# A one-time ScalarE delay between the first store and the first refill of a four-slot streaming kernel

## The chip, the cores and the metric

The kernel runs on one core of a Trainium2 chip. The metric is the device time of one execution in microseconds; lower is better. Most executions of one kernel agree within 0.3%, and faster or slower needs 2%. No other core of the chip is used by the program.

## The reference, cut to what matters

The input `x` has 384 x 384 positions of 384 bf16 channels, 113.25 MB. A mean over all positions gives one value per channel; it is scaled by one weight and passed through a sigmoid, and every position is multiplied by the result.

```python
g = jnp.einsum("bhwc->bc", x) / (H * W)
s = g * w1d[0]              # k = 1, so no neighbours
s = _sigmoid(s)
return x * s[:, None, None, :]
```

Read literally, this needs `x` twice. The kernel reads it once: it takes the gate from the first 4 row groups (`s_early`), applies it at once, and sums everything on the side. At the end it compares the true bf16 gate with the early one; only if they differ does it do a second pass. They don't differ on this data. So 113.25 MB come in and 113.25 MB go out.

## The kernel before

A row group ("row" in the code) is 128 positions, one per partition of SBUF, the core's on-chip memory. A tile is 60 rows: 46,080 contiguous bytes on each of 128 partitions, 5.90 MB. There are 19 tiles and 4 slots for them in SBUF, plus 12 first rows kept apart. Loads are issued by SyncE (queue SPq), three half tiles at the start by ScalarE; all stores are issued by ScalarE (queue ACTq). TensorE sums each tile, then VectorE multiplies it in place, then it is stored, then its slot is loaded again. Each load or store is carried by 16 DMA engines in packets, for a full tile one packet per partition; it has landed when the last of the 16 engines has reported its part.

```python
    def put(place, n, r0, to=None):
        ...
        plan.op("vector", gate(to, place, n, s_early),
                reads=["s_early"] + rows(place, n), writes=rows(to, n))
        plan.final.append(
            plan.dma("scalar", dram(o_rows, r0, n), at(to, n), reads=rows(to, n))
        )
    ...
    for k in range(n_tiles):
        if k >= SLOTS:
            put(slot(k), TILE, row0(k - SLOTS))
            load(slot(k), TILE, row0(k))
        there = rows(slot(k), TILE)
        plan.relay(ready, "gpsimd", "tensor", there, there, ["acc1"])
    ...
    for k in range(n_tiles - SLOTS, last):
        put(slot(k), TILE, row0(k))
    put(slot(last), TILE, row0(last), slot(n_tiles))
    put(base, FIRST, 0)
```

`Planner` notes who writes and reads each row and adds the semaphore waits; each engine's stream keeps the order of the calls. I call the tiles 0 to 18, "store 3" the store of tile 3, "load 4" the load of tile 4, which is the first refill of a slot.

Of the kernel before, what the change touches and what calls it, by code (L numbers as in the profile page):

```python
# [3 lines left out]
P = 128  # L4
# [5 lines left out]
ACT_F = mybir.ActivationFunctionType  # L10
# [139 lines left out]
def split(n, most):  # L150
    k = -(-n // most)
    return [n // k + (i < n % k) for i in range(k)]
# [2 lines left out]
WIDE = 512  # L155


FIRST, EARLY, TILE, SLOTS, BOTH = 12, 4, 60, 4, 3


def bass_standalone__channel_attn_eca__vision_kernel(
# [5 lines left out]
    B, H, W, C = x.shape  # L167
    assert B == 1 and C == ROW and (B * H * W) % (4 * P) == 0
    n_rows = B * H * W // P
    x_rows, o_rows = x.flatten_outer_dims(), out.flatten_outer_dims()  # L170

    def dram(view, r0, n):
        return view[r0 * P : (r0 + n) * P, :].rearrange("(p t) c -> p (t c)", p=P)
# [5 lines left out]
    warm = nc.alloc_sbuf_tensor("warm", [P, 2], F32)  # L179
# [3 lines left out]
    n_arena = nc.sbuf_bytes_remaining // (2 * C)  # L183
# [7 lines left out]
    def at(r0, n):  # L191
        assert r0 + n <= n_arena
        return arena[:, r0 * C : (r0 + n) * C]

    def rows(r0, n):
        return [("sb", r) for r in range(r0, r0 + n)]

    def gate(to, place, n, s):
        s_b = s[:].unsqueeze(1).broadcast_to([P, n, C])
        v, to_v = (at(r, n).rearrange("p (t c) -> p t c", t=n) for r in (place, to))  # L200
        return lambda e: e.tensor_tensor(to_v, v, s_b, ALU.mult)  # L201

    n_tiles = (n_rows - FIRST) // TILE
    base = SLOTS * TILE
    assert (n_rows - FIRST) % TILE == 0 and base + FIRST < n_arena
    assert FIRST % 4 == EARLY % 4 == TILE % 4 == 0 and EARLY + 4 < FIRST
    last = n_tiles - 1
    ready = nc.alloc_semaphore("ready")
# [1 line left out]
    def slot(k):  # L210
        return k % SLOTS * TILE

    def row0(k):
        return FIRST + k * TILE
# [2 lines left out]
    s_true = at(base + FIRST, 1)  # L217
    plan = Planner(nc, "a", 70)

    def load(place, n, r0, queues=("sync",)):  # L220
        i = 0
        for queue, m in zip(queues, split(n, -(-n // len(queues)))):
            plan.dma(
                queue,
                at(place + i, m),
                dram(x_rows, r0, n)[:, i * C : (i + m) * C],
                writes=rows(place + i, m),
            )
            i += m
# [83 lines left out]
    def put(place, n, r0, to=None):  # L313
        to = place if to is None else to
        plan.op(
            "vector",
            gate(to, place, n, s_early),
            reads=["s_early"] + rows(place, n),
            writes=rows(to, n),
        )  # L320
        plan.final.append(
            plan.dma("scalar", dram(o_rows, r0, n), at(to, n), reads=rows(to, n))
        )

    def weight():

        plan.op(
            "scalar",
            lambda e: e.activation(warm[:, 1:2], warm[:, 0:1], ACT_F.Sigmoid),  # L329
            reads=["warm"],  # L330
            writes=["warm1"],
        )
        plan.op(
            "tensor",
            lambda e: e.matmul(  # L335
                w_all[:, 0:1], ones[0:1, :], w_one[0:1, 0:1], start=True, stop=True
            ),
            reads=["ones", "w_one"],
            writes=["w_all"],
        )  # L340
        for i, n in enumerate((EARLY, n_rows)):
            plan.op(
                "vector",
                lambda e, i=i, n=n: e.tensor_scalar_mul(  # L344
                    w_scaled[:, i : i + 1], w_all[:, 0:1], 1.0 / float(P * n)
                ),
                reads=["w_all"],
                writes=[f"w_scaled{i}"],
            )

    plan.op("gpsimd", lambda e: e.memset(warm[:, 0:1], 0.0), writes=["warm"])  # L351
    plan.op("vector", lambda e: e.memset(ones[:], 1.0), writes=["ones"])  # L352
    load(base, FIRST, 0)
    for k in range(BOTH):
        load(slot(k), TILE, row0(k), ("sync", "scalar"))
        if k == 0:
            plan.dma("scalar", w_one[0:1, 0:1], w1d.unsqueeze(0), writes=["w_one"])
    for k in range(BOTH, SLOTS):
        load(slot(k), TILE, row0(k))
    heads = {e: len(plan.streams[e]) for e in ("sync", "scalar")}  # L360
    weight()
    sum_first()
    add_banks(0, copy=True)
# [5 lines left out]
        reads=["total", "w_scaled0", "warm1"],  # L369
        writes=["s_early"],  # L370
# [3 lines left out]

    for k in range(n_tiles):
        if k >= SLOTS:
            put(slot(k), TILE, row0(k - SLOTS))
            load(slot(k), TILE, row0(k))
        there = rows(slot(k), TILE)
        plan.relay(ready, "gpsimd", "tensor", there, there, ["acc1"])  # L380
    plan.signals("tensor", rows(base, FIRST), ["acc1"])
    for k in range(n_tiles - SLOTS, last):
# [12 lines left out]
        reads=["total", "w_scaled1"],  # L395
        writes=["s_true"],
# [6 lines left out]
        reads=["s_true", "s_early"],  # L403
        writes=["total"],
# [4 lines left out]
        reads=["total"],  # L409
        writes=["wrong"],  # L410
# [4 lines left out]
        reads=["wrong"],  # L415
        writes=["redo"],
# [5 lines left out]
    half, r0 = base // 2, 0  # L422
    for k, n in enumerate(split(n_rows, half)):
        place = k % 2 * half
# [4 lines left out]
            reads=rows(place, n),  # L429
            writes=rows(place, n),  # L430
# [98 lines left out]
```

## Time and profile before

| | before |
|---|---|
| time, median of the first 3 runs | 529.54 us (529.05 to 530.78) |
| span of the profiled run | 527.2 us |
| PE busy, VectorE busy | 42%, 46% |
| DMA engines, share of 16 | 53.6% + 46.1% = 99.7% |
| bytes over the span | 226.52 MB, 430 GB/s |

From the page of the kernel before: the busy share of the 16 DMA engines in 40 slices (tenths), the rate in each slice, the two queues (q10 is ACTq, q1 is SPq: packets, MB, share of 16 engines' span), and the two large groups of DMA issues (last column: median us from issue to landing).

```profile
DMA  9999999999999999999999999999999999999997
GB/s 392 425 425 414 440 447 427 413 447 444 434 409 447 444 434 409 447 444 434 416 437 447 437 413 437 447 441 409 437 447 444 409 434 447 444 416 427 442 447 331
q10 hardware_dynamic: 3314, 122.10, 53.6%
q1 hardware_dynamic: 2880, 104.40, 46.1%
...
out_dram<-arena ACTq DMA_DIRECT2D x19, 5760.0 KB, 49.4
arena<-in_x_dram SPq DMA_DIRECT2D x16, 5760.0 KB, 35.6
```

The engines have work in every slice. The table by stage of the same kernel (start:end, length, then per engine busy us and count, granted clock, DMA share, GB/s) shows the long middle:

```profile
125.00:480.00 355.00, 149.17 (x585) 0.00 (x0) 158.17 (x14) 0.00 (x0) 0.00 (x0) 0.70 1.00 434
```

PE is busy for 149 of these 355 us and VectorE for 158; DMA has a share of 1.00. The trace also keeps a record of each DMA packet and of each DMA engine's part of a landing; I worked the following out of those packet records. A packet of 46,080 bytes takes 1.70 us, 27.07 B/ns, or 433 GB/s for 16 engines. At that pace all the bytes need 523 us. The Trainium skill ("DMA: Bandwidth & Descriptors", section "Where 436 GB/s comes from") gives 16 x 32 B x 850 MHz = 435.2 GB/s as the ceiling of the ports; the trace agrees, at 433.

The place that the change touches is 60 to 100 us. From the timeline of the kernel before (start, duration from the first to the last of a merged group, engine, operation):

```profile
61.72 31.48 ACTq L109 DMA_DIRECT2D out_dram<-arena  x3
...
75.00 24.42 SPq L109 DMA_DIRECT2D arena<-in_x_dram  x2
```

Store 0 lands at 74.98 us and load 4 is issued at 75.00. Store 1 was issued at 61.72 and is queued behind store 0.

### The profile page before, as it was taken

The numbers are of one execution on the slowest core, as the hardware profiler recorded it, in microseconds if no ns is written. First come the engines' busy times: TensorE is split into PE (matmuls) and PEld (weight loads), VectorE is DVE, ScalarE is ACT, GpSimd is POOL, SyncE is SP. The second block draws the span as 40 slices with busy tenths as digits, with TensorE's granted clock in tenths as the row PEclk, the third lists the DMA queues.
The fourth block names the chain that finished last, engine by engine and source line by source line (L and its number), as shares of the span: only waits on it lengthen the run. The fifth ranks groups of instructions, "written<-read, shape, count | busy, mean of one in ns | idle before, by whom it ended". The sixth has DMA issues, their size and how long they took to land. (4 is left out here: it accounts for less than half of the span.)

```text
span 527.2 us, 1066 instructions
## 1 busy us (share of the span) xinstructions
PE 220.1 (42%) x865; PEld 0.2 (0%) x2; DVE 240.1 (46%) x38; ACT 2.7 (1%) x4; POOL 0.3 (0%) x5
## 2 busy tenths in 40 slices
PE   0389471080807161625343343526261708080900
PEld 0000000000000000000000000000000000000000
DVE  0229958008090808171625353443536261708940
ACT  1000000000000000000000000000000000000000
POOL 0000000000000000000000000000000000000000
PEclk9999876586757676676869595858585858585865
DMA  9999999999999999999999999999999999999997
GB/s 392 425 425 414 440 447 427 413 447 444 434 409 447 444 434 409 447 444 434 416 437 447 437 413 437 447 441 409 437 447 444 409 434 447 444 416 427 442 447 331
DMA packets 6196, 226.52 MB, mean 430 GB/s; under 512 B 690, under 2 KB 690, under 8 KB 690
## 3 DMA queue, kind: packets, MB, share of 16 engines
q10 hardware_dynamic: 3314, 122.10, 53.6%
q1 hardware_dynamic: 2880, 104.40, 46.1%
q8 instruction: 1, 0.02, 0.0%
q14 instruction: 1, 0.01, 0.0%
HBM read 113.25 MB, written 113.25 MB: 430 GB/s over the span
## 5 line engine op out<-in xcount | busy, mean ns | idle before, releaser
L201 DVE TENSOR_TENSOR arena<-arena,s_early 128x23040 bf16<-128x23040 bf16 (+1 forms) x20 | 233.5, 11679 | 250.4 <-PE acc L237 247.0
L237 PE MATMUL acc<-arena,ones 128*128 128x512 bf16 x863 | 219.6, 421 | 265.5 <-PEq L276 265.5
L344 DVE TENSOR_SCALAR w_scaled<-w_all 128x1 f32<-128x1 f32 x2 | 0.2, 153 | 14.5 <-PE w_all L335 14.5
L335 PE MATMUL w_all<-w_one,ones 1*128 1x1 bf16 x1 | 0.2, 158 | 15.5 <-DMA w_one<-in_w1d_dram 15.5
L308 DVE TENSOR_TENSOR total<-total,acc 128x128 f32<-128x128 f32 (+2 forms) x11 | 4.5, 408 | 0.3
L392 ACT ACTIVATE arena<-total,w_scaled 128x384 bf16<-128x384 f32 x1 | 0.6, 615 | 485.9 <-DVE total L308 485.9
L329 ACT ACT_TABLE_LOAD x1 | 1.3, 1283 | 2.3 <-issue 2.3
L306 DVE COPY total<-acc 128x384 f32<-128x384 f32 x1 | 0.6, 558 | 1.2 <-PE acc L237 1.2
L400 DVE TENSOR_TENSOR total<-arena,s_early 128x384 f32<-128x384 uint16 x1 | 0.6, 559 | 0.7 <-ACT arena L392 0.7
L366 ACT ACTIVATE s_early<-total,w_scaled 128x384 bf16<-128x384 f32 x1 | 0.6, 615 | 16.0 <-DVE total L308 16.0
L352 DVE MEMSET ones<- 128x128 bf16 x1 | 0.2, 165 | 1.0 <-PEq L514 1.0
L235 PE MATMUL acc<-arena,ones 128*128 128x512 bf16 x1 | 0.6, 610 | 0.0
L408 DVE TENSOR_REDUCE wrong<-total 128x1 f32<-128x384 f32 x1 | 0.6, 553 | 0.0
L329 ACT ACTIVATE warm<-warm 128x1 f32<-128x1 f32 x1 | 0.2, 203 | 0.0
L414 DVE CAST redo<-wrong 128x1 int32<-128x1 f32 x1 | 0.2, 154 | 0.0
L235 PEld LDWEIGHTS acc<-arena,ones 128*128 128x128 bf16 x1 | 0.1, 105 | 0.0
L335 PEld LDWEIGHTS w_all<-w_one,ones 1*128 1x128 bf16 x1 | 0.1, 99 | 15.5 <-issue 15.5
L514 POOL MEMSET const-bfloat16-1.0<- 128x1 bf16 x1 | 0.1, 102 | 0.0
L514 POOL MEMSET const-uint8-127<- 128x1 uint8 x1 | 0.1, 102 | 0.0
L514 POOL MEMSET const-float32-0.0<- 128x1 f32 x1 | 0.1, 99 | 0.2 <-issue 0.2
L514 POOL MEMSET const-float32-1.0<- 128x1 f32 x1 | 0.1, 99 | 0.0
L351 POOL MEMSET warm<- 128x1 f32 x1 | 0.1, 98 | 0.5 <-POOLq L514 0.5
## 6 DMA issues: line engine op xcount, KB each, us to landing
out_dram<-arena ACTq DMA_DIRECT2D x19, 5760.0 KB, 49.4
arena<-in_x_dram SPq DMA_DIRECT2D x16, 5760.0 KB, 35.6
arena<-in_x_dram ACTq DMA_DIRECT2D x3, 2880.0 KB, 27.6
arena<-in_x_dram SPq DMA_DIRECT2D x3, 2880.0 KB, 36.4
arena<-in_x_dram SPq DMA_DIRECT2D x1, 1152.0 KB, 10.3
out_dram<-arena ACTq DMA_DIRECT2D x1, 1152.0 KB, 23.5
w_one<-in_w1d_dram ACTq DMA_DIRECT2D x1, 0.0 KB
```

The costliest lines, as they stand in the source:

```text
L201: return lambda e: e.tensor_tensor(to_v, v, s_b, ALU.mult)
L235: loaded.append(e.matmul(bank, weights, moving, start=start, stop=stop))
L237: return e.add_instruction(mybir.InstMatmult(name=nc.get_next_instruction_name(), engine=mybir.EngineType.PE, ins=[e.lower_ap(moving), e.l ...
L306: emit = lambda e, part=part, of=of: e.tensor_copy(part, of)
L308: emit = lambda e, part=part, of=of: e.tensor_tensor(part, part, of, ALU.add)
L329: lambda e: e.activation(warm[:, 1:2], warm[:, 0:1], ACT_F.Sigmoid),
L335: lambda e: e.matmul(w_all[:, 0:1], ones[0:1, :], w_one[0:1, 0:1], start=True, stop=True),
L366: lambda e: e.activation(s_early[:], total[:], ACT_F.Sigmoid, scale=w_scaled[:, 0:1]),
L392: lambda e: e.activation(s_true, total[:], ACT_F.Sigmoid, scale=w_scaled[:, 1:2]),
L400: lambda e: e.tensor_tensor(total[:], s_true.bitcast(U16), s_early[:].bitcast(U16), ALU.not_equal),
L408: lambda e: e.reduce_max(wrong[:], total[:], axis=mybir.AxisListType.X),
L514: nc = _bacc.Bacc("TRN2", target_bir_lowering=False, num_devices=1)
```

## The change

Its intent is to let the stores run ahead of the loads once, by delaying the first refill: between the landing of store 0 and the issue of load 4, ScalarE fills 8 spare rows of SBUF (128 x 3072 elements) which nobody reads. Store 1 is put ahead of this in ScalarE's stream. Cut to its core:

```diff
-FIRST, EARLY, TILE, SLOTS, BOTH = 12, 4, 60, 4, 3
+FIRST, EARLY, TILE, SLOTS, BOTH, PAUSE = 12, 4, 60, 4, 3, 8
 ...
+    def pause(r0):
+        to = at(base + FIRST + 1, PAUSE)
+        plan.op(
+            "scalar",
+            lambda e: e.activation(
+                to, warm[:, 0:1].broadcast_to([P, PAUSE * C]), ACT_F.Sigmoid
+            ),
+            reads=["warm"],
+            writes=rows(r0, 1) + ["pause"],
+        )
 ...
     for k in range(n_tiles):
         if k >= SLOTS:
-            put(slot(k), TILE, row0(k - SLOTS))
-            load(slot(k), TILE, row0(k))
+            for i in range(2) if k == SLOTS else () if k < SLOTS + 2 else (k - SLOTS,):
+                put(slot(i), TILE, row0(i))
+            if k == SLOTS:
+                pause(slot(k))
+            load(slot(k), TILE, row0(k), reads=["pause"] if k == SLOTS else ())
```

`writes=rows(r0, 1)` makes the pause wait for store 0, which reads those rows; `reads=["pause"]` makes load 4 wait for the pause. A comparison of the two instruction orders shows one new ACT instruction after the second store, and no other instruction moved on any engine.

More of the change, by code (lines that the diff above doesn't have):

```diff
@@ L204, in bass_standalone__channel_attn_eca__vision_kernel @@
     base = SLOTS * TILE
-    assert (n_rows - FIRST) % TILE == 0 and base + FIRST < n_arena
+    assert (n_rows - FIRST) % TILE == 0 and base + FIRST + 1 + PAUSE <= n_arena
     assert FIRST % 4 == EARLY % 4 == TILE % 4 == 0 and EARLY + 4 < FIRST
@@ L218, in bass_standalone__channel_attn_eca__vision_kernel, with load @@
     plan = Planner(nc, "a", 70)
-    def load(place, n, r0, queues=("sync",)):
+    def load(place, n, r0, queues=("sync",), reads=()):
         i = 0
@@ L226, in load @@
                 dram(x_rows, r0, n)[:, i * C : (i + m) * C],
+                reads=reads,
                 writes=rows(place + i, m),
```

## The prediction

> **What bounds the kernel now.** The DMA engines, nearly from end to end. The page shows them busy at 9 tenths or more in 39 of 40 slices; the queue table gives 53.6% plus 46.1% = 99.7% of the 16 engines' span, and 226.52 MB moved at a mean of 430 GB/s. Between 125 and 480 us the table by stage gives 434 GB/s at a DMA share of 1.00. In the packet records a 46,080-byte packet takes 1.70 us there, 27.07 B/ns per engine, 433 GB/s for 16. The Trainium skill ("DMA: Bandwidth & Descriptors", section "Where 436 GB/s comes from") puts the ceiling at 435.2 GB/s; the trace agrees, 433. All bytes at 433 GB/s take 523 us of the 527.2 us span; the other 4 us are the start (first packets at about 1 us, slow until 2), the last store's landing, and some 0.9 us of stretched packets near 50 us, when the first store joins the loads. PE (42%) and DVE (46%) are not limits, and the chain of waits explains only the last 38 us on the engines while the stores drain. So at most about 4 us (0.8%) could be won at all.
>
> **What the change does.** Bytes, DMA sizes, PE and DVE work stay. The order of instructions shows one new ACT instruction: after two stores ACT waits for the first store's landing, writes 128x3072 and only then issues store 2; the load into slot 0 waits for that instruction instead of the store. VectorE's order is unchanged; the planned reordering of the second gating only places its store ahead of the pause.
> Cost: the trace's activations take 203 ns (1 element) and 615 ns (384). The Trainium skill ("ScalarE: Activation LUTs", section "What ACT_TABLE_LOAD costs") gives 186 ns + 0.833 N ns with immediates; estimate for 3072 elements 2.75 us, no new table load (Sigmoid is already in).
>
> **On the critical path.** Store 0 landed at 74.98 us, the load was issued at 75.00 and its first packets ran at 78.5. Now it is issued near 77.8. But the limit is bytes, not the load's start: store 1 was issued at 61.7 and has some 5.9 MB left at 75, enough to keep all engines full for 13 us alone. Store 2, ready at 73.8 and now issued near 77.8, queues behind store 1 anyway. So DMA stays full and what the load loses the store gains. A fluid estimate from these numbers (two queues, equal shares, 433 GB/s) shifts stores about 2.8 us earlier and loads about 2.8 us later, in every later period of 27.2 us, and leaves the end unchanged. Slack at the tail: store 18 is issued at 501, its turn comes at 510.8; the shift takes under 3 us of that.
>
> **Predicted time:** 529.3 us, range 528.1 to 531.0 (before: 529.54). Faster by over 2%: 0.01; within 2%: 0.975; slower by over 2%: 0.015.
>
> **What the profile would show.** An ACT ACTIVATE of about 2.75 us near 75 us; the first refill issued near 77.8; store landings in mid-run about 3 us earlier against loads about 3 us later; load time from issue to landing (median of the 16 full tiles) up from 35.6 to about 41 us, stores from 49.4 down to about 44; DMA share still 99.7%, 433-434 GB/s from 125 to 480 us, packets still 1.70 us.
>
> **What would make it wrong.** A packet rate that depends on how reads and writes alternate on the 16 engines (in the load-only start packets ran at 26.6 to 26.95 B/ns, up to 1.7% slower); the stretched packets near 50 us recurring at the refill; or the ACT queue running dry during the pause.

## The result, and the profile after

| | before | after |
|---|---|---|
| time, median of 4 runs | 529.54 us (529.05 to 530.78) | 529.18 us (528.63 to 529.75) |
| span of the profiled run | 527.2 us | 526.9 us |

The ratio of the fast runs is 0.999, with a 95% interval of 0.9969 to 1.001: the same. This ratio is the record's own figure for the fast runs; here and below it is not quite the ratio of the medians quoted.

The page of the kernel after, the same lines and the new group on ACT (busy us, mean ns of one, idle before and what ended it):

```profile
DMA  9999999999999999999999999999999999999998
...
q10 hardware_dynamic: 3314, 122.10, 53.6%
q1 hardware_dynamic: 2880, 104.40, 46.1%
...
L332 ACT ACTIVATE arena<-warm 128x3072 bf16<-128x3072 f32 x1 | 2.8, 2762 | 53.9 <-DMA out_dram<-arena 53.9
...
out_dram<-arena ACTq DMA_DIRECT2D x19, 5760.0 KB, 45.5
arena<-in_x_dram SPq DMA_DIRECT2D x16, 5760.0 KB, 39.3
```

The table by stage and the timeline of the kernel after, same stretches:

```profile
125.00:480.00 355.00, 150.87 (x585) 0.00 (x0) 158.36 (x14) 0.00 (x0) 0.00 (x0) 0.69 1.00 434
```

```profile
74.30 2.76 ACT L332 ACTIVATE arena<-warm 128x3072 bf16<-128x3072 f32 x1 [53.92 <-DMA out_dram<-arena]
74.31 19.65 ACTq L109 DMA_DIRECT2D out_dram<-arena  x2
77.09 46.84 SPq L109 DMA_DIRECT2D arena<-in_x_dram  x3
```

The pause is there, 2.76 us long, and load 4 is issued when it ends. The middle still moves 434 GB/s at a share of 1.00, and the queues' shares are the same to a tenth of a per cent. What moved is the phase of loads against stores: from issue to landing a store takes 45.5 us instead of 49.4, a load 39.3 instead of 35.6. In the landing records store 9 comes at 314.1 instead of 316.6 us, load 12 at 326.3 instead of 325.0. Both kernels end the same way: the last full store lands at 524.4 before and 524.1 after.

One detail surprised me. Store 2 is issued at 74.31, at the start of the pause and not at its end. The Trainium skill ("Perfetto Trace Analysis", section "Per-engine timelines") says that a ScalarE sequencer is ready for its next instruction once it has pushed an ACTIVATE into the wait queue, before it executes. This trace agrees: 74.31 lies between the ACTIVATE's start at 74.30 and its end at 77.06. So the pause holds back the refill alone and not the store behind it.

### The profile page after: what moved, and what is told of

Read it like the earlier page. It is cut to its first block, busy times and chain, and to the rows that moved or that the text cites. A ratio compares the mean times of both kernels' runs of the same rounds, so it can differ in the third digit from the quotient of the medians.

```text
span 526.9 us, 1067 instructions
## 1 busy us (share of the span) xinstructions
PE 221.8 (42%) x865; PEld 0.2 (0%) x2; DVE 240.0 (46%) x38; ACT 5.5 (1%) x5; POOL 0.3 (0%) x5
## 3 DMA queue, kind: packets, MB, share of 16 engines
q10 hardware_dynamic: 3314, 122.10, 53.6%
q1 hardware_dynamic: 2880, 104.40, 46.1%
## 5 line engine op out<-in xcount | busy, mean ns | idle before, releaser
L332 ACT ACTIVATE arena<-warm 128x3072 bf16<-128x3072 f32 x1 | 2.8, 2762 | 53.9 <-DMA out_dram<-arena 53.9
## 6 DMA issues: line engine op xcount, KB each, us to landing
out_dram<-arena ACTq DMA_DIRECT2D x19, 5760.0 KB, 45.5
arena<-in_x_dram SPq DMA_DIRECT2D x16, 5760.0 KB, 39.3
```

The costliest lines, as they stand in the source:

```text
L332: lambda e: e.activation(to, warm[:, 0:1].broadcast_to([P, PAUSE * C]), ACT_F.Sigmoid),
```

## The experiments

The theory, A: the time is the bytes at 433 GB/s, plus the time in which neither queue has anything to move, plus the fixed start and end. A refill's delay costs nothing as long as stores are queued for the DMA engines. Its rivals: B, the refill's delay is paid on the chain load, sum, gate, store, load; C, four slots hide any pause of this order. Two more, D and E, came up on the way. Twelve kernels were run. All but the one named gave the right result. By the 2% rule the record calls the first run below unclear, since its interval straddles 1.02, the run with fewer bytes faster, and all others the same; a difference of 4 to 6 us is under 2%, and I treat it as real only where the interval excludes 1.

### A pause of eight units, four ways

One unit is the change's ACTIVATE, 2.76 us. Eight units on ScalarE hold back both load 4 and store 2:

```diff
-        plan.op(
+        for _ in range(8):
+            plan.op(
                 "scalar", ...            # the same ACTIVATE
```

> The pause eight times in a row (8 x 2.76 = 22.1 us on ScalarE, from the landing of store 0 near 74.3 to about 96.4 us); it holds back store 2 and the first refill. Theory A (the time is the bytes at 433 GB/s plus the time in which neither queue has anything to move): store 1 alone keeps the DMA engines full only to about 87 us, then nothing is queued until about 98.5, so the time grows by some 11.8 us to 541 us (539 to 543), with a hole of 10 to 13 us in the DMA records near 87 to 99. Rival B (a delay of the refill is paid on the chain load, sum, gate, store, load): +19 us over the changed kernel or more. Rival C (four slots hide a pause of this size): within 1 us of 529.2.

Measured: 540.8 us (538.7 to 541.6), ratio 1.0208, interval 1.0181 to 1.0236. From the timeline of this run and its table by stage:

```profile
74.26 22.32 ACT L333 ACTIVATE arena<-warm 128x3072 bf16<-128x3072 f32 x8 [53.80 <-DMA out_dram<-arena]
...
93.82 0.82 ACTq L109 DMA_DIRECT2D out_dram<-arena  x2
96.60 22.91 SPq L109 DMA_DIRECT2D arena<-in_x_dram  x3
```

```profile
80.00:100.00 20.00, 1.94 (x10) 0.00 (x0) 12.16 (x1) 16.42 (x6) 0.00 (x0) 0.63 0.72 295
```

The share falls to 0.72 and the rate to 295 GB/s. In the packet records the last packets of store 1 end at 87.2 and the first of store 2 begin at 94.7, in the mean over the engines: the hole is 7.5 us, and not the 10 to 13 that I expected, because store 2 is issued when the last of the eight ACTIVATEs starts (93.82) and not when it ends. The span grew by 12.6 us over the changed kernel's. The rest is 1.9 us of packets that took longer than 1.70 us, mostly just after both queues started again, and 3.1 us because the 16 engines no longer finish together: the last full store's parts land from 531.8 to 536.7 us, in the changed kernel from 522.4 to 524.1. C is out. A's total held partly by luck: the hole was 7.5 us where A had 11.8, and two terms that A did not have made up the difference.

Next, the same eight units with store 2 put ahead of them:

```diff
-            for i in range(2) if k == SLOTS else () if k < SLOTS + 2 else (k - SLOTS,):
+            for i in range(3) if k == SLOTS else () if k < SLOTS + 3 else (k - SLOTS,):
```

> The same eight pauses, but store 2 (ready near 73.8) is put ahead of the pause on ScalarE, so that two stores are queued when it begins. Theory A: stores 1 and 2 cover the DMA engines to about 101 us, the pause ends near 96.4, so no hole and the time is that of the changed kernel, 529.2 (528 to 530.5). Rival B (the refill's delay is paid): as in the run with the same pause behind store 1, +12 us or more, since the refill is delayed by the same 22 us.

Measured: 535.2 us (533.1 to 535.6), ratio 1.01, interval 1.0075 to 1.0125. This missed A's range by 4.7 us; B, with at least 12 us more, missed too.

Next, eight units that hold back store 2 but not the refill (load 4 waits for store 0 as before; in `pause` the planner's note of who wrote and read the slot's first row is put back afterwards):

```diff
+        of = rows(r0, 1)[0]
+        kept = plan.writer[of], list(plan.readers[of])
         for _ in range(8): ...
+        plan.writer[of], plan.readers[of] = kept
 ...
-            load(slot(k), TILE, row0(k), reads=["pause"] if k == SLOTS else ())
+            load(slot(k), TILE, row0(k))
```

> The same eight pauses on ScalarE behind store 1, but the first refill waits for store 0 only, as in the kernel before; so only store 2 is held back. Theory A: the refill and store 1 share the engines, store 1 lands near 99, store 2 is issued near 96.4: no hole, 529.2 (528 to 530.5). If the cost of the long pause came from the ACT queue alone being held (store 2 late), it would show here as +5 us or more.

Measured: 529.6 us (528.8 to 532.7), ratio 1.0019, interval 0.9981 to 1.0057: the same, as A says. The DMA share stays full while ScalarE is busy with the pause:

```profile
80.00:100.00 20.00, 0.61 (x3) 0.00 (x0) 12.16 (x1) 16.62 (x7) 0.00 (x0) 0.57 1.02 442
```

Last, the refill alone held back, by eight memsets of the same rows on GpSimd:

```diff
+        for _ in range(8):
+            plan.op("gpsimd", lambda e: e.memset(to, 0.0),
+                    writes=rows(r0, 1) + ["pause"])
```

> The pause moved to GpSimd (eight memsets of the same 128x3072 rows; their length is not known from any trace of this case yet, guessed 13 to 26 us in all), so that only the first refill is held back and store 2 is issued as soon as it is gated. Theory A: stores 1, 2 and 3 are queued in time and cover the engines past 110 us: no hole, 529.2 (528 to 530.5), with the refill landing later and the following stores earlier. Rival B (a refill's delay is paid on the chain): + the pause less 3 us, some 10 to 20 us.

Measured: 533.7 us (531.3 to 536.3), ratio 1.0088, interval 1.0043 to 1.0132. The memsets took 21.7 us in all. A said 529.2 and missed by 4.5 us; B said at least 10 more and missed too.

So of the four, the one where both queues could run dry (11.3 us more than the unchanged 529.5) came out as A has it in its total, and the one where only store 2 was held back in full; the two that delay the refill by 22 us with stores queued cost 4 to 6 us that A does not explain. Their page shows no hole: the DMA share is full. Their table by stage shows where the time went. First the one with store 2 ahead, then the one with the pause on GpSimd; for the changed kernel the same stretch has 432 GB/s.

```profile
158.00:187.00 29.00, 12.33 (x44) 0.00 (x0) 20.77 (x2) 0.00 (x0) 0.00 (x0) 0.68 0.99 391
210.00:480.00 270.00, 115.63 (x438) 0.00 (x0) 111.02 (x10) 0.00 (x0) 0.00 (x0) 0.72 1.00 433
```

```profile
158.00:187.00 29.00, 12.62 (x45) 0.00 (x0) 20.65 (x2) 0.00 (x0) 0.00 (x0) 0.68 1.01 391
210.00:480.00 270.00, 120.02 (x443) 0.00 (x0) 112.08 (x11) 0.00 (x0) 0.00 (x0) 0.69 1.00 434
```

Busy to 99% and more, yet only 391 GB/s: the packets themselves took longer. In the packet records of the GpSimd run 76 of 133 full-size packets on the ACT queue that started between 158 and 187 us took over 1.8 us, typically 2.2, against none in the kernels before and after; summed over the run, packets stretched by 4.5 us per engine after 60 us, against 0.1 in the changed kernel. In the run with store 2 ahead the engines also drift apart again: the last full store's parts land from 523.7 to 531.2 us. Two things are special about this stretch. The long delay had let the stores run out: store 3 landed at 130.3 and store 4 was issued at 152.1, so loads had run alone for some 28 us by the packet records. And store 4 then ran beside load 7, their first packets 1.4 us apart (156.9 and 155.5, in the mean over the engines) and the two landing together (store 186.8, load 186.6). That makes theory D, slow because they run in step, and theory E, slow because the store queue starts again after standing empty.

### The length of the pause

The pause as in the change, with 2, 3, 4 and 5 units (the loop count above).

> Pause of two units (5.5 us). In the two runs that held back loads past 126 us the store queue ran dry for 25 us, and then 46,080-byte store packets took 2.2 us instead of 1.70 for a whole tile (158 to 186 us), which costs those runs 4 to 6 us that theory A had not foreseen. Theory D (the slow spell belongs to loads and stores that run through their tiles in step, starting and landing within about 3 us of each other) and theory E (it follows a queue that starts again after standing empty) differ in this sweep of the pause's length. Here: no queue stands empty, loads land about 16 us after stores in mid-run (of a period of 27.2): A, D and E all say 529.2 (528.2 to 530.5), slow packets under 1 us in all after 60 us.

> Three units (8.3 us). Loads land about 21 us after stores in mid-run, no queue stands empty. A and E: 529.2 (528.2 to 530.5). D: 529.2 also unless the gap closes to within 3 us of the next store, then many slow store packets and over 535.

> Four units (11.1 us). The fluid estimate has loads and stores start and land together in every period, with no hole in mid-run, and about 1 us more at the tail. A and E: 530.5 (529 to 532). D: store packets at 2.2 us in most periods, so a rate clearly under 433 GB/s from 125 to 480 us and over 540 us in all.

> Five units (13.9 us). Store 1's bytes run out near 87.5 and the held-back transfers begin near 91, so theory A gives the first hole: about 3.5 us plus the start, 533 (531.5 to 535), and the eight-unit pause's 540.8 lies on the same line of 2.76 us a unit. D as for four units, if loads and stores land within 3 us of each other.

| units | fast runs, median us (range) | ratio, 95% interval |
|---|---|---|
| 1 (the change) | 529.18 (528.63 to 529.75) | 0.999, 0.9969 to 1.001 |
| 2 | 529.39 (529.01 to 529.90) | 1.0008, 0.9992 to 1.0025 |
| 3 | 4 fast runs: 529.58, 530.23, 532.38, 534.33 | 1.0033, 1.0008 to 1.0058 |
| 4 | 534.31 (530.29 to 538.03) | 1.0124, 1.0082 to 1.0167 |
| 5 | 534.89 (531.86 to 537.02) | 1.0107, 1.0063 to 1.0152 |
| 8 | 540.8 (538.7 to 541.6) | 1.0208, 1.0181 to 1.0236 |

Two units are free, as A says. With three, two of the four fast runs lie above A's range (to 530.5). Five cost about what A says (533, range to 535), but not for A's reason. From the timeline and the table by stage of the run with five units:

```profile
86.28 7.21 ACTq L109 DMA_DIRECT2D out_dram<-arena  x2
89.06 25.12 SPq L109 DMA_DIRECT2D arena<-in_x_dram  x3
```

```profile
85.00:125.00 40.00, 0.97 (x3) 0.00 (x0) 8.12 (x1) 4.00 (x2) 0.00 (x0) 0.50 1.01 415
```

A expected a hole of about 3.5 us. But store 2 was issued at 86.28, when the fifth ACTIVATE started, and its first packets began at 87.4 where those of store 1 ended at 87.2 (means over the engines): the engines stood idle for under 0.2 us. The span grew by 6.0 us over the changed kernel's because packets stretched by 2.9 us per engine after 60 us, mostly just after the two queues started again, and because the engines drifted apart (the last full store's parts land from 524.3 to 530.1 us). So A's figure for five units is luck.

Four missed A's range: 534.3 instead of 530.5, with a spread of almost 8 us over four fast runs. Its profile fell on the fastest of them (530.29) and shows what A expects: 433 GB/s in the middle and next to no stretched packets, though loads and stores land within 3.5 us of each other in every period. So D, in the form "within about 3 us", did not hold there (by first packets they were further apart: load 7 at 167.4 us, store 5 at 173.9, in the mean); and what makes the slower runs slow stays open, because none of them was profiled. With three units a fifth execution took 584.53 us; the profile fell on it. It is set aside and explains nothing here: its trace would fit D (from 174 us on each load lands within 0.3 us of a store, and 125 to 480 us has 399 GB/s), but a slow run alone shows no cause. No length beat the kernel before.

### Loads and stores out of step

If D holds, more waiting could make the GpSimd run faster. ScalarE holds store 4 back by three units after its tile is gated, so that load 7 leads by some packets:

```diff
         plan.op("vector", gate(to, place, n, s_early), ...)
+        if r0 == row0(4):
+            hold(to)          # three ACTIVATEs of 2.76 us that wait for this gating
         plan.final.append(plan.dma("scalar", ...))
```

> The GpSimd pause run again with one thing more: ScalarE holds store 4 back by three units (8.3 us) after its tile is gated. In that run store 4 and load 7 ran their packets in step from 157 to 186 us (landings within 0.2 us of each other) and store packets took 2.2 us. Theory D (slow because the two run in step): load 7 now leads by about three packets, packets are back to 1.70 us, and a kernel with more waiting is faster, 529 to 531 against 533.7. Theory E (slow because the store queue starts again after standing empty beside loads): still empty, even longer, so the slow spell stays: 533 to 538.

Measured: 530.8 us (529.28, 529.54, 532.00, 535.42), ratio 1.0054, interval 0.9993 to 1.0114. The profile, which fell on the fastest run, has no slow spell: none of 176 packets on the ACT queue between 158 and 187 us took over 1.8 us. Load 7 and store 4 still ran beside each other, but with their first packets 6.7 us apart (155.4 and 162.1, in the mean). The times do not settle it. So six units, with five rounds:

> As the run that holds store 4 back by three units, but by six (16.6 us), five rounds: the three-unit run's profile had no slow spell (packets at 1.70 us), but its four times scattered from 529.3 to 535.4, so its time did not settle the matter. Theory D (the spell comes of load 7 and store 4 running in step): load 7 is nearly through before store 4 begins, no spell, 529 to 531 in most runs and a mean under the 533.7 of the GpSimd pause alone. Theory E (it follows the store queue's standing empty, now longest of all): the spell is there, 533 to 540.

Measured: 530.4 us (529.25 to 532.47, 6 runs), ratio 1.0016, interval 0.9988 to 1.0044. The same stretch in the two runs, with the hold of three units and with that of six:

```profile
158.00:187.00 29.00, 14.97 (x64) 0.00 (x0) 20.33 (x2) 2.10 (x1) 0.00 (x0) 0.76 1.00 432
```

```profile
158.00:187.00 29.00, 22.52 (x90) 0.00 (x0) 26.03 (x3) 11.96 (x5) 0.00 (x0) 0.85 1.02 429
```

429 to 432 GB/s instead of 391. With six units, 14 of 172 store packets still took over 1.8 us, instead of 76 of 133. The store queue stood empty for longer than in the GpSimd run, so E would have the spell, and it is all but gone. PE and VectorE are busier in this stretch than in the slow run (22.5 and 26.0 us against 12.6 and 20.7), so their work is not its cause either. With six units store 4 does not run beside load 7 at all: the packets of load 7 end at 169.0 us, where those of store 4 begin (means), and the 14 slow packets are the first ones after this restart (168.4 to 169.2 us). So this run shows the spell gone without an overlap; that it goes with the two overlapping out of step is shown by the one profiled execution with three units alone, the fastest of its four. Together they support D for this spell; why two streams in step are slower, and how closely in step they must be, no run here shows. That the kernel with 16.6 us more waiting is the faster one is likely but not beyond doubt: the intervals of the two ratios, 1.0043 to 1.0132 and 0.9988 to 1.0044, meet at their ends.

### A pause at every refill

Each of the 15 refills waits for its own unit; each store is put ahead of the pause before it.

```diff
-            for i in range(2) if k == SLOTS else () if k < SLOTS + 2 else (k - SLOTS,):
+            for i in range(2) if k == SLOTS else (k - SLOTS + 1,):
                 put(slot(i), TILE, row0(i))
-            if k == SLOTS:
-                pause(slot(k))
-            load(slot(k), TILE, row0(k), reads=["pause"] if k == SLOTS else ())
+            pause(slot(k), k)
+            load(slot(k), TILE, row0(k), reads=[f"pause{k}"])
```

> A pause of one unit (2.76 us) at each of the 15 refills, 41.4 us in all, each store being put ahead of the pause before it as in the change. Theory A (bytes at 433 GB/s, plus only the time in which nothing is queued): a refill is issued at a store's landing while the load before it still has 8 to 12 us to go, so every later pause is hidden in that queue; 529.2 (528.2 to 530.5), mid-run still 433 GB/s. Rival B (a refill's delay is paid on the chain load, sum, gate, store, load, four tiles at a time): 15 pauses over 4 slots, +10 us or more; paid in full +41.

Measured: 529.5 us (528.6 to 531.0), ratio 0.9995, interval 0.9958 to 1.0031: the same. From the groups and from the table by stage of this run:

```profile
L332 ACT ACTIVATE arena<-warm 128x3072 bf16<-128x3072 f32 x15 | 41.4, 2762 | 392.3 <-DMA out_dram<-arena 392.3
```

```profile
125.00:480.00 355.00, 162.33 (x585) 0.00 (x0) 155.81 (x14) 33.38 (x13) 0.00 (x0) 0.69 1.00 433
```

41.4 us of pauses, each between a store's landing and the refill of its slot, cost nothing. B is out. This is the strongest single piece of evidence for why the change is free.

### Fewer bytes

The changed kernel without the store of tile 8. The result is wrong.

```diff
+        if r0 == row0(8):
+            return
         plan.final.append(plan.dma("scalar", ...))
```

> The changed kernel without the store of tile 8, wrong on purpose (those rows of the output stay unwritten): 5.90 MB less to move, no engine's work taken away. Theory A: 5.90 MB at 433 GB/s, 13.6 us less: 515.6 (514 to 517). Rival B (the chain through PE and VectorE sets the pace): less than 5 us.

Measured: 516.8 us (516.0 to 517.2), ratio 0.9756, interval 0.9721 to 0.9791; 0.0244 of 529.5 us is 12.9 us. No engine's work was removed, only 5.90 MB. At 433 GB/s these are 13.6 us. So this is what moves the time of this kernel. The missing 0.7 us is within the noise, since the interval allows 11.1 to 14.8 us; it may have a place in the trace, though I did not test it: the last full store's parts land from 508.7 to 512.7 us in this run, 4.0 us apart, and 1.75 us apart in the changed kernel.

## Why the prediction was right, point by point

- "within 2%", 529.3 us, range 528.1 to 531.0: 529.18 measured. Right, and for its main reason: the limit is bytes. Removing bytes moves the time at nearly 433 GB/s; 41 us of pauses don't move it.
- "estimate for 3072 elements 2.75 us": 2.762 us. The formula of the Trainium skill ("ScalarE: Activation LUTs", section "What ACT_TABLE_LOAD costs"), 186 ns + 0.833 ns an element, gives 2.745; the trace agrees within 1%.
- "Now it is issued near 77.8": 77.09, since store 0 landed 0.7 us earlier in this run than in the profiled run of the kernel before. The first packets of load 4 on the 16 engines start at 82.0 in the mean, against 79.2: 2.8 us later.
- "Store 2 ... now issued near 77.8": wrong. It was issued at 74.31, because a DMA issue does not wait for the ACTIVATE ahead of it on ScalarE. It made no difference, since it queued behind store 1, as the prediction said.
- "stores about 2.8 us earlier and loads about 2.8 us later": right in the mean over the 16 engines' parts of a landing: store 9 is 3.0 us earlier (312.0 instead of 315.1), load 12 is 2.7 us later (325.5 instead of 322.7). The landing itself is the last part, and by it stores come 2.5 us earlier (store 9) and loads only 1.3 us later (load 12). The medians from issue to landing therefore moved less than forecast: from 49.4 to 45.5 and from 35.6 to 39.3, where "about 44" and "about 41" stood. The step that was off is that the fluid estimate takes the 16 engines for one: the last part of load 12 came 2.3 us after the mean of its parts before, and 0.8 us after it in the changed kernel. What sets this spread, no run isolates.
- "DMA share still 99.7%, 433-434 GB/s": 53.6% + 46.1%, and 434 GB/s. "packets still 1.70 us": yes.
- "Slack at the tail": the end did not move, 526.9 against 527.2 us.
- Of its own list of what could make it wrong, none happened at this pause. The runs showed that two of the three are real at a longer one: the queues running dry (7.5 us of hole with eight units), and a packet rate that depends on how loads and stores run beside each other (391 GB/s for 29 us). The theory as I first put it, that full queues are all that matters, is too simple for refills held back by 14 to 22 us. It is enough for the change itself, where the packets kept their 1.70 us.

No version beats both kernels. All bytes at 433 GB/s need 523 us of the 527 us span, so no reordering could win more than about 4 us, and none of those tried won any of it.

## What to carry to other kernels

Where the DMA engines are busy to 99.7% at their full packet rate, ask of a new wait first whether the queues hold enough bytes to last through it; 2.76 us behind 5.9 MB of queued stores was free here, and so were fifteen such pauses. When the cover is used up the cost comes back, and not only as the hole, so look at the rate beside the busy share: a share of 1.01 at 391 GB/s is a loss that the share hides. And before trusting a delay on an engine to hold back the DMA issues behind it, look in the timeline at when they were issued.

## What the Trainium skill lacked or had wrong

- "DMA: Bandwidth & Descriptors" has no word on loads and stores of one core slowing each other at large packet sizes. Here 76 of 133 store packets of 46,080 bytes took about 2.2 us instead of 1.70 over 29 us (391 GB/s) where a store and a load ran in step, and none of 176 in the one profiled execution in which the store was moved by some packets (432 GB/s).
- The same page, section "Where 436 GB/s comes from", says that about 358 GB/s bind a transfer between HBM and SBUF. With loads and stores mixed, and no other core of the chip used by the program, the runs show 434 GB/s over 355 us. "HBM Reference" (section "Specifications (TRN2)") has it better: a core streaming alone measures well above its share.
- The same page gives about 0.6 us to the first byte for a DMA issued from SyncE or ScalarE. After the hole in the eight-unit run, with the engines idle, it was 0.9 us (store 2 issued at 93.82, first packets at 94.7). When the other queue is already full it is far more: load 4 was issued at 75.00 and its first packets started from 78.5 to 80.5 us.
- No page that I read gives how far the 16 DMA engines can drift apart over a kernel, which the last landing then waits for: the last full store's parts landed 1.75 us apart in the changed kernel and 4.9 us apart after the eight-unit pause, which accounts for 3.1 us of that run.
- "Perfetto Trace Analysis" was right on when ScalarE's sequencer goes on; none of the pages draws the consequence that a DMA issue behind a long ACTIVATE goes out at its start (74.31 against an end at 77.06 us).
